# The start flag in place of a memset for the forward attention's accumulators

## The chip, the cores and the metric

The kernel runs on one core of a Trainium2 chip. The metric is the device time of one execution in microseconds (us). A ratio below is the mean time of one kernel's fast runs over that of the other's of the same rounds, with a 95% interval; so it is not quite the ratio of the medians that are quoted. The engines are PE (TensorE: matmuls, in program order), PEld (its weight loads), DVE (VectorE), ACT (ScalarE) and POOL (GpSimd). PSUM is the memory that the matmuls write, here the tile `accbank`, and a bank is one part of it; the start flag is a matmul's argument `start`. In the profile's timeline a row runs on over idle gaps under 0.15 us.

## The reference, cut to what matters

The whole is one transformer block, forward and backward: layer norm, attention with 32 heads of 16 columns over 2048 rows, an MLP, and the gradients. The change touches the forward attention alone:

```
qkv = (x @ wqkv).reshape(B, S, 3, H, Dh) ...        # S = 2048, H = 32, Dh = 16
p = softmax(einsum('bhqd,bhkd->bhqk', q, k) * scale)
o = einsum('bhqk,bhkd->bhqd', p, v)
```

## The kernel before

The forward works in 64 units: 4 chunks of 512 queries x 16 pairs of heads. A unit has 16 steps, one for each block of 128 keys. From one unit to the next there are 63 changes, which are numbered below. A step makes the score tile `st` on PE, the exponential `pu` on ACT, and, two steps later, the value product: eight matmuls that add `pu` times `Vaug` into eight groups of 17 columns (2 heads x 4 blocks of queries; column 17 sums the weights). After the last step DVE reads the unit out. Background work (projections, the MLP) is mixed in on PE between the steps.

```python
accp = self.open_pool("fwacc", bufs=1, space=PSUM)
accbank = accp.tile([P, 2, 2, 4, DH + 1], F32, name="accbank")    # two halves of one tile
...
def pv(u):
    (qc, g, jp, kb, acc, pu) = u
    if kb == 0:
        nc.vector.memset(acc, 0.0)
    for a in range(2):
        h = 4 * g + 2 * jp + a
        for sub in range(4):
            nc.tensor.matmul(acc[:, a, sub, :], lhsT=pu[:, a, sub * P:(sub + 1) * P], rhs=Vaug[:, kb, h, :],
                             start=False, stop=False, skip_group_check=True)
    if kb < ST - 1:
        return
    st0 = 4 * qc
    for a in range(2):                                            # the readout: four DVE instructions
        h = 4 * g + 2 * jp + a
        nc.vector.reciprocal(self.rl[:, st0:st0 + 4, h], acc[:, a, :, DH])
        nc.vector.tensor_tensor(O32[:, :, h * DH:(h + 1) * DH], acc[:, a, :, 0:DH],
                                self.rl[:, st0:st0 + 4, h:h + 1].to_broadcast([P, 4, DH]), ALU.mult)
    if (g, jp) == (NQ - 1, 1) and qc < SC - 1:
        bg.add(self.gen_mlp(qc, self.take_o(qc, O32)))            # four casts on DVE, then the MLP
...
for n, (qc, g, jp) in enumerate(order):
    acc = accbank[:, n % 2]
    for kb in range(ST):
        ...
        nc.tensor.matmul(stt[:, a, :], ...)                       # a = 0, 1: the scores
        nc.scalar.activation(pu[:], stt[:], ACT.Exp, scale=self.scale)
        pend.append((qc, g, jp, kb, acc, pu))
        if len(pend) > 2:
            pv(pend.pop(0))
        bg.step(1.08 if qc else 1.15)                             # background matmuls
```

The softmax here doesn't subtract the row's maximum and nothing guards it: scores larger than these inputs give would overflow.

## Time and profile before

| | kernel before |
|---|---|
| median of three runs | 3085.02 us (3082.49 to 3086.32) |
| time and span of the profiled run (not one of the three) | 3071.37 and 3069.6 us |
| first to last value matmul (start to start) | 110.2 to 1149.8 us |
| PE idle before a value matmul, for the memset | 64.1 us, 63 times |
| ACT idle before an exponential | 84.4 us |

The next lines are the view of busy time by stretches, for two stretches in the middle and at the end of the forward. Each engine's busy us has its count of instructions behind it; the last three columns are PE's granted clock, the DMA engines' busy share and GB/s.

```profile
370.00:650.00 280.00, 252.24 (x3064) 140.78 (x3117) 83.47 (x253) 263.10 (x283) 52.83 (x91) 0.98 0.37 91
900.00:1155.00 255.00, 229.44 (x2699) 125.90 (x2747) 76.84 (x238) 231.53 (x249) 43.66 (x76) 0.98 0.25 71
```

ACT (the fourth pair) is busy 263.10 of 280 us, 94%; the 17 us that it stands still there are what a change in this stage can win. DVE, on which the memset runs, is busy 30%.

### The profile page before, as it was taken

What the parts mean: (1) busy time and instruction counts of PE and PEld (TensorE: products, weight loads), DVE (VectorE), ACT (ScalarE), POOL (GpSimd) and SP (SyncE); (2) the same over time, 40 slices, a digit from 0 to 9 for tenths busy, and PEclk for the clock granted to TensorE, in tenths of its full rate; (3) what the DMA queues carried; (4) which work ended last, traced back from release to release, by engine and by line L of the source; (5) the groups of instructions that cost most, each with busy time, mean ns of one, the idle gap of its engine ahead of it and who ended that gap; (6) DMA issues with size and microseconds to landing.
All of it is one profiled execution on the core that took longest, in us unless ns stands there. A gap on an engine that the chain in (4) does not pass through costs nothing. (4 is left out here: it accounts for less than half of the span.)

```text
span 3069.6 us, 72394 instructions
## 1 busy us (share of the span) xinstructions
PE 2731.8 (89%) x29893; PEld 1417.4 (46%) x30394; DVE 1822.7 (59%) x2661; ACT 2240.1 (73%) x3322; POOL 396.6 (13%) x646
## 2 busy tenths in 40 slices
PE   3689889989998988589999999999999999999796
PEld 1345445544444543454444444444444444444343
DVE  5322123322322334367888888888888888888575
ACT  3489999999999984106777777777777777777443
POOL 2343111320221122571000000000000000000000
PEclk7899999999999999799999999999999999999898
DMA  3974230531351136888999999999999999999942
GB/s 128 212 166 121 65 88 25 141 80 37 93 114 48 54 99 183 177 195 164 188 205 200 188 204 189 201 194 192 205 191 206 195 194 206 188 188 180 235 128 72
DMA packets 1306719, 471.12 MB, mean 153 GB/s; under 512 B 1237074, under 2 KB 1269844, under 8 KB 1306388
## 3 DMA queue, kind: packets, MB, share of 16 engines
q1 hardware_dynamic: 1277476, 378.87, 65.7%
q0 software_dynamic: 28384, 86.01, 9.1%
q8 instruction: 238, 3.90, 0.5%
q10 hardware_dynamic: 528, 1.57, 0.1%
q14 instruction: 93, 0.76, 0.1%
HBM read 88.87 MB, written 67.64 MB: 51 GB/s over the span
## 5 line engine op out<-in xcount | busy, mean ns | idle before, releaser
L1185 ACT ACTIVATE pu<-st 128x512 bf16<-128x512 f32 x2048 | 1132.7, 597 | 361.0 <-PE st L1183 297.4
L1190 DVE TENSOR_TENSOR ds<-dp,pu 128x1024 bf16<-128x1024 f32 x1024 | 1208.1, 1219 | 232.9 <-ACT pu L1185 225.0
L361 ACT ACTIVATE pu<-st 128x1024 bf16<-128x1024 f32 x1024 | 956.8, 1047 | 84.4 <-PE st L358 80.4
L1183 PE MATMUL st<-KTm,QTq 128*128 128x512 bf16 x2048 | 778.3, 380 | 13.3 <-ACT pu L1185 11.5
L1133 PEld LDWEIGHTS <-dsT 128*128 128x128 bf16 x8192 | 486.7, 96 | 489.6 <-DMA dsT<-ds 20.2
L1186 PE MATMUL dp<-VTm,dOTq 128*128 128x512 bf16 x1779 | 672.6, 378 | 7.4 <-DVE ds L1190 6.0
L358 PE MATMUL st<-QTm,KTq 128*128 128x512 bf16 x1937 | 596.0, 384 | 57.9 <-issue 17.4
L1133 PE MATMUL accq<-Kg,dsT 128*128 128x16 bf16 x8192 | 493.2, 170 | 27.8 <-DMA dsT<-ds 13.5
L328 PEld LDWEIGHTS <-pu 128*128 128x128 bf16 x8192 | 355.7, 96 | 326.1 <-issue 95.9
L328 PE MATMUL accbank<-Vaug,pu 128*128 128x17 bf16 x8192 | 359.3, 171 | 70.0 <-DVE accbank L324 64.1
L1113 PE MATMUL acckv<-ds,Qg 128*16 128x512 bf16 x2048 | 308.3, 381 | 0.9 <-DVE ds L1190 0.7
L1113 PE MATMUL acckv<-pu,dOg 128*16 128x512 bf16 x2048 | 308.3, 381 | 0.0
L1183 PEld LDWEIGHTS <-QTq 128*128 128x128 bf16 x2048 | 195.9, 96 | 220.8 <-issue 215.8
L358 PEld LDWEIGHTS <-KTq 128*128 128x128 bf16 x2048 | 194.7, 97 | 214.7 <-issue 165.4
L1186 PEld LDWEIGHTS <-dOTq 128*128 128x128 bf16 x2048 | 197.3, 96 | 38.0 <-DVE ds L1190 16.2
L1044 POOL DMA_DIRECT2D wqkv<-in_A_wqkv_dram x1 | 0.8, 788 | 1493.1 <-DMA dsT<-ds 1493.1
L464 DVE TENSOR_SCALAR ev_fm<-pps,bcol 128x512 bf16<-128x512 f32 x60 | 45.0, 750 | 156.7 <-PE pps L456 88.7
L335 DVE RECIPROCAL rl<-accbank 128x4 f32<-128x4 f32 x128 | 23.0, 179 | 175.3 <-PE accbank L328 175.3
L309 POOL DMA_DIRECT2D QTm<-QTq_d x128 | 64.9, 510 | 450.0 <-PE st L358 406.4
L914 DVE TENSOR_SCALAR rT<-pps,bias 128x512 bf16<-128x512 f32 x42 | 31.5, 750 | 116.9 <-PE pps L911 116.7
L922 DVE SCALAR_TENSOR_TENSOR auT<-pps,rT 128x512 bf16<-128x512 f32 x42 | 29.0, 691 | 86.1 <-PE pps L920 71.0
L456 PE MATMUL pps<-xhat1T,wpad 128*128 128x512 bf16 x223 | 78.8, 393 | 0.3 <-issue 0.2
(313 smaller groups left out, 2125.1 us busy)
## 6 DMA issues: line engine op xcount, KB each, us to landing
KTq<-KTq_d POOLq DMA_DIRECT2D x32, 512.0 KB, 3.6
duT_d<-auT POOLq DMA_DIRECT2D x4, 1792.0 KB, 8.2
aT_d<-rT POOLq DMA_DIRECT2D x4, 1792.0 KB, 12.7
QTq_d<-ev_fm SPq DMA_DIRECT2D x32, 128.0 KB, 2.1
QTm<-QTq_d POOLq DMA_DIRECT2D x128, 32.0 KB, 2.0
KTq_d<-ev_fm SPq DMA_DIRECT2D x32, 128.0 KB, 2.0
VTq_d<-vT POOLq DMA_DIRECT2D x4, 1024.0 KB, 6.3
O_d<-O POOLq DMA_DIRECT2D x4, 1024.0 KB, 7.1
```

Of the source, the lines that this page charges most:

```text
L309: nc.gpsimd.dma_start(QTm[j][32 * j:32 * j + 32, :], self.QTq_d[g, 32 * j:32 * j + 32, 512 * qc:512 * (qc + 1)])
L328: nc.tensor.matmul(acc[:, a, sub, :], lhsT=pu[:, a, sub * P:(sub + 1) * P], rhs=Vaug[:, kb, h, :], start=False, stop=False, skip_group_che ...
L358: nc.tensor.matmul(stt[:, a, :], lhsT=KT[:, kb * P:(kb + 1) * P], rhs=QTm[2 * jp + a][:], start=True, stop=True)
L361: nc.scalar.activation(pu[:], stt[:], ACT.Exp, scale=self.scale)
L456: nc.tensor.matmul(pt[:], lhsT=self.wpads[t][:, kt, g, :], rhs=self.xhat1T[:, kt, s0:s0 + 512], start=(kt == 0), stop=(kt == DT - 1))
L464: nc.vector.tensor_scalar(ev[:], pt[:], bc, None, ALU.add)
L1113: nc.tensor.matmul(acckv[r:r + DH, :], lhsT=T[n][:, ib, col:col + DH], rhs=src[:, a, :], start=(ib == 0), stop=(ib == ST - 1))
L1133: nc.tensor.matmul(accq[:, ib, a, :], lhsT=dsT[:, (i * 2 + a) * 4 + sub, :], rhs=T["K"][:, 4 * c + sub, col:col + DH], start=(c == 0 and i ...
L1183: nc.tensor.matmul(stt[:], lhsT=T["QT"][:, q], rhs=masked["KT"][2 * jp + a][:, c0:c0 + 512], start=True, stop=True)
L1185: nc.scalar.activation(pu[:, a, :], stt[:], ACT.Exp, scale=self.scale)
L1186: nc.tensor.matmul(dp[:, a, :], lhsT=T["dOT"][:, q], rhs=masked["VT"][2 * jp + a][:, c0:c0 + 512], start=True, stop=True)
L1190: nc.vector.tensor_tensor(dsg[:, i], dp[:], pu[:], ALU.mult)
```

## The change

The intent is to drop the memset and let the first matmul of a unit, which carries the start flag, overwrite instead of adding.

```diff
         def pv(u):
             (qc, g, jp, kb, acc, pu) = u
-            if kb == 0:
-                nc.vector.memset(acc, 0.0)
             for a in range(2):
                 h = 4 * g + 2 * jp + a
                 for sub in range(4):
                     nc.tensor.matmul(acc[:, a, sub, :], lhsT=pu[:, a, sub * P:(sub + 1) * P], rhs=Vaug[:, kb, h, :],
-                                     start=False, stop=False, skip_group_check=True)
+                                     start=(kb == 0 and a == 0 and sub == 0), stop=False, skip_group_check=True)
```

## The prediction

> **What bounds the kernel now.** I read the page's forty slices first, to see whether the stage that the change touches has one limit.
>
> ```profile
> PE   3689889989998988589999999999999999999796
> DVE  5322123322322334367888888888888888888575
> ACT  3489999999999984106777777777777777777443
> ```
>
> The forward attention is slices 2 to 14, about 108 to 1150 us. There ACT is at 9 tenths nearly throughout, PE at 8 to 9, and DVE only at 1 to 3. So DVE's busy time is no cost in this stage, and removing DVE work can only pay where somebody waits for it. The backward stage after it (slices 18 to 37) is not touched; it can only start earlier or later. The next view is the groups by line, for 90 to 1155 us; its columns are operation, count, busy us and mean ns, then idle time before and what ended it.
>
> ```profile
> L361 ACT ACTIVATE pu<-st 128x1024 bf16<-128x1024 f32 x1024 | 956.8, 1047 | 84.4 <-PE st L358 80.4 <-ACT pu L361 0.5 <-remote 0.5
> L328 PE MATMUL accbank<-Vaug,pu 128*128 128x17 bf16 x8192 | 359.3, 171 | 70.0 <-DVE accbank L324 64.1 <-issue 0.4
> L336 DVE TENSOR_TENSOR O<-accbank,rl 128x64 f32<-128x64 f32 x128 | 28.4, 222 | 3.4 <-DVE rl L335 0.2
> L335 DVE RECIPROCAL rl<-accbank 128x4 f32<-128x4 f32 x128 | 23.0, 179 | 175.3 <-PE accbank L328 175.3
> L324 DVE MEMSET accbank<- 128x136 f32 x64 | 11.0, 172 | 5.9 <-DVE Vaug L441 0.2
> ```
>
> The reader should see three things. The exponentials (L361) are 956.8 us of a stage of some 1040 us: ACT is the limit, 14.95 us for each of the 64 head-pair units. ACT is idle for only 84.4 us before them, and 80.4 of that waits for the score matmuls (L358). And PE idles 64.1 us, in 63 of the 64 units, before the first value matmul of a unit (L328), waiting for the memset. PE works in program order, so while it stands at that matmul it cannot make the next score tile, and ACT runs dry. The 64.1 us looks like the prize. The timeline of one change of units shows that it is not.
>
> ```profile
> 617.19 0.23 DVE L336 TENSOR_TENSOR O<-accbank,rl 128x64 f32<-128x64 f32 x1
> 617.52 0.17 DVE L324 MEMSET accbank<- 128x136 f32 x1
> 617.74 0.35 PE L328 MATMUL accbank<-Vaug,pu 128*128 128x17 bf16 x8 [0.43 <-DVE accbank L324]
> ...
> 618.85 14.92 ACT L361 ACTIVATE pu<-st 128x1024 bf16<-128x1024 f32 x16 [0.35 <-PE st L358]
> ```
>
> Columns: start, length, engine, line, operation; in brackets the idle time before and its releaser. The memset is the last of five DVE instructions in a chain: PE ends the old unit, then reciprocal, multiply, reciprocal, multiply read it out, then the memset clears the other half of the same tile, then PE goes on. The last multiply ends at 617.42, the memset at 617.69, PE starts at 617.74. ACT then idles 0.35 us and runs 16 exponentials without a gap. This is the repeating pattern: one ACT bubble per unit, caused here.
>
> **What the Trainium skill says.** PSUM — Partial Sum Buffer, section The four PSUM rules: a matmul with the start flag clears the written bits of its whole 2 KiB bank on the quadrants it writes, and a later matmul without it overwrites where the bit is clear and adds where it is set. The accumulator tile is 2 halves x 136 fp32 = 1088 bytes, so both halves lie in one bank; one start flag per unit therefore prepares all eight 17-column groups, and the other half is already complete, because PE runs the units in order. So the result should stay right with no added matmul. The same page, section PSUM bank collisions raise a hardware error: two engines must not touch one bank and quadrant at once, even at different columns. Hence the new unit's first matmul must still wait until DVE has finished reading the old unit in the other half. The trace before agrees with ordering by the whole tile: the first reciprocal reads only head 0's half of the columns but starts after all eight matmuls of both heads; and the memset of the second unit, which clears a half that nobody has used, did not run in DVE's free time between 99.6 and 111.1 us but at 127.60, after the first unit's multiplies, while later work such as L855 was moved far ahead. Perfetto Trace Analysis, section Per-instruction lifecycle, says that a DVE record ends at the write acknowledgement, with the semaphore's travel after it. The trace fits: memset end to PE start is 0.05 us. I expect the same 0.05 after the multiply.
>
> **The change, part by part.** Removed: 64 memsets of 172 ns, 11.0 us of DVE busy time, worth nothing as such. Added: a flag on 64 of the 8192 matmuls; the shape stays 128x17, so no time. Moved: PE's wait, from the memset to the last multiply before it. What the path gains per unit is from the multiply's end to the memset's end: 617.69 - 617.42 = 0.27 us, of which 0.17 is the memset and 0.10 the gap between two DVE instructions. I took this difference for all 63 units from the timeline of DVE. In 53 it is 0.26 to 0.28 us. In ten it is 0.38 to 1.86 us, as other DVE work stands between: at the ends of the first three query chunks four casts (L865) of the finished output do.
>
> ```profile
> 379.24 1.62 DVE L865 CAST O_b<-O 128x512 bf16<-128x512 f32 x4
> ...
> 380.88 0.17 DVE L324 MEMSET accbank<- 128x136 f32 x1
> ...
> 381.11 0.36 PE L328 MATMUL accbank<-Vaug,pu 128*128 128x17 bf16 x8 [2.01 <-DVE accbank L324]
> ```
>
> Here PE waits 2.01 us and would be free of the casts: 1.85 us gained. The others sit behind one to three layer-norm or copy steps.
>
> Not each gain reaches the end: ACT is the limit, so PE's gain counts only as far as ACT was idle after it. For each unit I therefore took the smallest of three: the gain, PE's recorded wait, and ACT's idle time in the three microseconds after the memset. In 8 units ACT did not idle at all (0.43 us of PE wait was hidden by the two buffered score tiles); they give 0. The ten large ones give 10.8 us together. The other 45 give 12.2 us, some 0.27 each. Sum: 23.0 us. The recorded ACT idle time in these places is 61.6 us, so some 39 us of it stays: the two reciprocals and multiplies and whatever delays them.
>
> **Rivals.** (a) The wait is taken off altogether: if nothing orders the new half against reading the old one, up to the whole 64.1 us of PE wait goes, and of ACT's idle time up to 61.6 us: 3085 - 61.6 = 3023.4 us, exactly at the border of 2%. For it: the halves are disjoint in columns. Against it: the two signs of tile-wide ordering above, and the collision rule. I give it 4%. (b) ACT is the limit and the wait is hidden anyway: then about 0. For it: 8 units show precisely that, and ACT's digits are 9. Against it: a bubble of 0.35 us or more after most of the other memsets. A weaker form, where a third of the 0.27 us is given back to another wait, makes the gain some 15 us. (c) A new order: with the memset gone, the layout of other instructions on DVE and GpSimd may shift, so that a multiply lands behind a 0.7 us background operation more often; PE's long waits now (6.03 us at 193.38, 3.37 at 155.97, 3.10 at 957.10) come from late multiplies, not from the memset, and could grow or shrink by several us. This is noise of perhaps 8 us either way. (d) The earlier stage collides with DMA: I think not, as the DMA share is 0.25 to 0.37 between 370 and 1155 us.
>
> **Range and chances.** 3085.0 - 23.0 = 3062.0. Taking something off for given-back time (b), I predict 3064 us, -0.7%. With (c)'s 8 us and (b)'s weaker form, 3051 to 3077 should hold it 8 times in 10. Two per cent is 61.7 us, more than the sum by far; only (a) comes near. Slower by 2% would need a new wait of 1 us in every unit; nothing on PE was added.
>
> **What would show it.** Right: no L324 records; the same PE idle before L328, now released by the multiply (L336), about 64.1 - 25.2 = 39 us in total, where 25.2 is the sum of the gains bounded by PE's wait alone; a common wait of 0.16 instead of 0.43 us; ACT idle before L361 down from 84.4 to about 61; the backward stage unchanged in length. Wrong: PE's wait before L328 vanishing (rival a); ACT's idle time unchanged although PE's wait fell (b); multiplies standing behind other DVE work, with waits of over 1 us in more units than before (c).

## The result, and the profile after

The changed kernel takes 3055.51 us median (3054.82 to 3059.33, four runs) against 3084.86 us: ratio 0.9908 (0.9891 to 0.9925). The result is correct with one start flag for eight groups. On a second chip job it was 3054.74 against 3077.71 us, ratio 0.992, and on a third 3052.24 against 3077.98 us, ratio 0.9917; these two ran on one chip. So it is 23 to 29 us faster.

The groups by line of the changed kernel, 90 to 1155 us; the lines of the code are two lower than before (L359 was L361, L326 was L328, L334 was L336, L333 was L335):

```profile
L359 ACT ACTIVATE pu<-st 128x1024 bf16<-128x1024 f32 x1024 | 955.9, 1050 | 58.8 <-PE st L356 53.6 <-ACT pu L359 0.5 <-remote 0.5
L326 PE MATMUL accbank<-Vaug,pu 128*128 128x17 bf16 x8192 | 359.0, 171 | 47.1 <-DVE O L334 38.6 <-DVE lnb_nc L971 2.4 <-issue 0.7
L334 DVE TENSOR_TENSOR O<-accbank,rl 128x64 f32<-128x64 f32 x128 | 28.5, 222 | 3.1
L333 DVE RECIPROCAL rl<-accbank 128x4 f32<-128x4 f32 x128 | 23.0, 180 | 177.7 <-PE accbank L326 177.7
```

There is no memset row. PE's wait has a new releaser, the multiply of the readout (L334), and fell from 64.1 to 38.6 us; the 2.4 us put down to L971 (a small layer-norm step on DVE right behind the multiply) belong to it too, which makes 41.0. ACT's idle time fell from 84.4 to 58.8 us, by 25.6. The value matmul is 171 ns as before.

The same change of units as the prediction showed (the 31st), now in the changed kernel: the last multiply, PE's first value matmul of the new unit, and ACT's row over this stretch. Below it is ACT's busy time in 4 us around this change (stretch, length, busy us with the count, then the granted clock and the DMA's share and GB/s), first in the kernel before, then in the changed one.

```profile
607.43 0.23 DVE L334 TENSOR_TENSOR O<-accbank,rl 128x64 f32<-128x64 f32 x1
...
607.71 0.35 PE L326 MATMUL accbank<-Vaug,pu 128*128 128x17 bf16 x8 [0.16 <-DVE O L334]
...
589.09 34.65 ACT L359 ACTIVATE pu<-st 128x1024 bf16<-128x1024 f32 x37
```

```profile
616.00:620.00 4.00, 3.65 (x5) 1.00 0.43 125
606.00:610.00 4.00, 3.92 (x5) 1.00 0.43 124
```

The multiply ends at 607.66 and PE starts 0.05 us later; PE's wait is 0.16 instead of 0.43 us. ACT's row of 37 exponentials runs from 589.09 to 623.74 us, but it hides a short gap: ACT is busy 3.92 of 4 us where it was busy 3.65. So the bubble of 0.35 us at this change shrank to 0.08 us, by the same 0.27 us as PE's wait; it is not gone. In all 63 changes of this trace PE starts 0.05 to 0.06 us after the end of the last multiply.

At the end of a query chunk the four casts (here L863) now run beside PE:

```profile
375.06 0.23 DVE L334 TENSOR_TENSOR O<-accbank,rl 128x64 f32<-128x64 f32 x1
375.31 1.62 DVE L863 CAST O_b<-O 128x512 bf16<-128x512 f32 x4
...
375.33 0.35 PE L326 MATMUL accbank<-Vaug,pu 128*128 128x17 bf16 x8 [0.15 <-DVE O L334]
```

The wait here was 2.01 us and is 0.15 us. And the stretch of 280 us in the middle of the forward:

```profile
370.00:650.00 280.00, 259.84 (x3159) 145.14 (x3217) 81.56 (x238) 270.29 (x291) 52.84 (x91) 0.99 0.37 92
```

ACT is busy 270.29 of 280 us instead of 263.10, and PE gets 95 matmuls more done in the same time.

From the first value matmul's start to the last one's, the forward takes 1013.0 us (110.9 to 1123.9) instead of 1039.6, 26.6 us less. The profiled span fell by 16.1 us only. One reason is that the profiled run of the kernel before, 3071.37 us, was 11 us faster than the fastest timed one of that job (3082.49 us). Within the two traces, the difference lies between the stages: from the last value matmul to the first DVE step of the backward stage (the first `ds`) it is 251.6 us before and 257.9 after; from there to the span's end, 1668.2 and 1671.7. Over all traces that part between the stages varies from 251 to 262 us, so I take these few microseconds for scatter of single traces and judge the kernels by their timed runs.

### The profile page after: what moved, and what is told of

The parts are those of the page before. It is cut to its first block, busy times and chain, and to the rows that moved or that the text cites. A ratio compares the mean times of both kernels' runs of the same rounds, so it can differ in the third digit from the quotient of the medians.

```text
span 3053.5 us, 72311 instructions
## 1 busy us (share of the span) xinstructions
PE 2735.2 (90%) x29893; PEld 1420.6 (47%) x30394; DVE 1814.1 (59%) x2597; ACT 2238.9 (73%) x3322; POOL 396.4 (13%) x646
## 5 line engine op out<-in xcount | busy, mean ns | idle before, releaser
L359 ACT ACTIVATE pu<-st 128x1024 bf16<-128x1024 f32 x1024 | 955.9, 1050 | 58.8 <-PE st L356 53.6
L326 PEld LDWEIGHTS <-pu 128*128 128x128 bf16 x8192 | 355.4, 96 | 302.5 <-issue 71.9
L326 PE MATMUL accbank<-Vaug,pu 128*128 128x17 bf16 x8192 | 359.0, 171 | 47.1 <-DVE O L334 38.6
L333 DVE RECIPROCAL rl<-accbank 128x4 f32<-128x4 f32 x128 | 23.0, 180 | 177.7 <-PE accbank L326 177.7
```

## The experiments

All ten runs were correct, and each stands beside runs of the kernel before on the same chip.

**1. The change again.** Comment lines keep the line numbers; the code is the change's.

> The change again (line numbers kept by comment lines), to get its time against the kernel before on one chip, with more rounds. Theory (the start of the first value matmul moves from the memset's end to the last multiply's end): about 3055 us, ratio 0.991, PE idle before the value matmuls 41 us against 64 us. Rival (part of the 29 us was a better draw of the chip, since the profiled spans differ by 16 us only): ratio 0.994 to 0.995.

Measured: 3054.74 us (3052.11 to 3056.06) against 3077.71; ratio 0.992 (0.9904 to 0.9935). PE idle 42.3 us (39.9 + 2.4). So 0.991 is inside and 0.994 just outside the interval: the gain is real in timed runs, though the kernel before was 7 us faster here than in the first job, so that part of the first job's 29 us stays unconfirmed.

**2. The flag without the gain.** The flag is set and the memset stays.

```diff
-                                     start=False, stop=False, skip_group_check=True)
+                                     start=(kb == 0 and a == 0 and sub == 0), stop=False, skip_group_check=True)
```

> The start flag is set but the memset stays; the order of instructions on all five engines is that of the kernel before. Theory: as before, ratio 1.000 within 0.2%, PE idle before L328 64 us, released by the memset. Rival (the flag makes the matmuls cheaper, or overwriting instead of adding does): some of the 29 us is gained, ratio below 0.997, the 128x17 matmul under 171 ns.

Measured: 3078.99 us, ratio 0.9998 (0.9984 to 1.0013); the matmul is 171 ns; PE waits 60.3 us for the memset. The flag by itself gains nothing. Since the order of instructions is the same as before, this trace is also a second trace of the kernel before for every purpose of time: the two differ by 3.8 us in PE's wait and by 4.4 us in the length of the forward.

**3. The memset kept, but ahead of what stood between.**

```diff
-            if kb == 0:
+            if kb == 0 and (qc, g, jp) == order[0]:
                 nc.vector.memset(acc, 0.0)
...
+            if (qc, g, jp) != order[-1]:
+                nc.vector.memset(accbank[:, (order.index((qc, g, jp)) + 1) % 2], 0.0)
             if (g, jp) == (NQ - 1, 1) and qc < SC - 1:
```

> The kernel before with each memset issued right behind the last multiply of the unit before, ahead of the casts and of the background work that stood between in ten units; no flag; otherwise the same order on all engines. Theory (53 units cost 0.27 us each, ten cost more through what stands between): the ten units' excess over 0.27 us is gained, 10.8 - 10 x 0.27 = some 8 us: ratio 0.9974, 3077 us; PE idle before L328 about 55 us. Rival (the memset itself costs all, what stands between is hidden): ratio 1.000.

Measured: 3069.44 us, ratio 0.9972 (0.9956 to 0.9988). The time is as expected (with a wide interval: 3.7 to 13.5 us gained), PE's wait fell less: to 58.5 us. The trace says why: of the ten units, the three with casts went from 2.01, 2.00 and 1.85 to 0.43, 0.44 and 0.28 us and one other from 2.18 to 1.52, while the remaining six kept their waits, as the placing of DVE's instructions still put a background step ahead of the memset there. So the casts in front of the memset cost 1.6 us each, and PE's wait on them was not hidden.

**4. The memset twice.**

```diff
-            if kb == 0:
+            for _ in range(2 if kb == 0 else 0):
                 nc.vector.memset(acc, 0.0)
```

> The kernel before with each memset done twice, so that the chain is 0.2 to 0.27 us longer in all 63 units. Theory (the chain of readout and memset sets when ACT gets its next score tile, and each tenth of a microsecond of it counts): 55 to 63 units x 0.2 to 0.27 us = 11 to 17 us more, ratio 1.0036 to 1.0055, PE idle before L328 about 77 to 81 us. Rival (the wait is mostly hidden behind ACT, and the change gained elsewhere): under 4 us, ratio below 1.0013.

One change of units, with the last multiply, both memsets and PE's restart:

```profile
938.97 0.23 DVE L336 TENSOR_TENSOR O<-accbank,rl 128x64 f32<-128x64 f32 x1
939.29 0.45 DVE L324 MEMSET accbank<- 128x136 f32 x2
...
939.79 0.35 PE L328 MATMUL accbank<-Vaug,pu 128*128 128x17 bf16 x8 [0.70 <-DVE accbank L324]
```

From the multiply's end (939.20) to the second memset's end (939.74) it is 0.54 us; with one memset it was 0.27. Each memset thus costs the chain 0.27 us, not its 172 ns, and PE's wait of 0.43 became 0.70. In sum PE waits 83.2 us, 21 more than the mean of the two traces with one memset (62.2). Measured time: 3105.77 us (3090.89 to 3112.26), ratio 1.0084 (1.0063 to 1.0105): 28 us more by the medians. That is more than the expected 17. ACT's idle time is 102.4 us against their mean of 82.1, so 20.3 of the 21.0 us reached ACT. The profiled run, the fastest of the six at 3090.89 us, has a forward 20 us longer than the mean of those two traces (1057.9 against 1037.4). The other five were 13 to 21 us slower than it and have no trace; their granted clock was 0.962 to 0.965 against its 0.969, which may be why, but nothing here shows it. The rival (hidden) falls.

**5. The change a third time**, as the base for the next three.

> The changed kernel once more, as the base for the three runs beside it on this chip. Ratio to the kernel before 0.991 to 0.992.

Measured: 3052.24 us, ratio 0.9917 (0.9901 to 0.9934); PE's wait 44.4 us, ACT's idle time 55.3 us.

**6. A shorter readout on top of the change.**

```diff
-            for a in range(2):
-                h = 4 * g + 2 * jp + a
-                nc.vector.reciprocal(self.rl[:, st0:st0 + 4, h], acc[:, a, :, DH])
-                nc.vector.tensor_tensor(O32[:, :, h * DH:(h + 1) * DH], acc[:, a, :, 0:DH],
-                                        self.rl[:, st0:st0 + 4, h:h + 1].to_broadcast([P, 4, DH]), ALU.mult)
+            h = 4 * g + 2 * jp
+            rlv = self.rl[:, st0:st0 + 4, h:h + 2].rearrange("p s a -> p a s")
+            nc.vector.reciprocal(rlv, acc[:, :, :, DH])
+            nc.vector.tensor_tensor(O32[:, :, h * DH:(h + 2) * DH].rearrange("p s (a d) -> p a s d", a=2), acc[:, :, :, 0:DH],
+                                    rlv.unsqueeze(3).to_broadcast([P, 2, 4, DH]), ALU.mult)
```

> The changed kernel, with the readout of both heads in one reciprocal and one multiply instead of two each. Theory (what is left of PE's wait is the readout chain): the chain is some 0.3 to 0.35 us shorter, and the smallest of that, PE's wait and ACT's idle time, summed over the units of the changed kernel's trace, is 7.9 to 9.0 us: ratio to the changed kernel 0.997, PE idle before the value matmuls some 42 - 20 = 22 to 30 us. Rival (in most units the wait is hidden behind ACT by now, and the long ones come from other DVE work in front): under 3 us.

The groups of this kernel (90 to 1160 us) and one readout:

```profile
L361 ACT ACTIVATE pu<-st 128x1024 bf16<-128x1024 f32 x1024 | 951.6, 1054 | 40.8 <-PE st L358 36.1 <-remote 2.2 <-ACT pu L361 0.5
L328 PE MATMUL accbank<-Vaug,pu 128*128 128x17 bf16 x8192 | 358.1, 171 | 22.5 <-DVE O L336 16.0 <-issue 0.2
...
601.23 0.21 DVE L335 RECIPROCAL rl<-accbank 128x8 f32<-128x8 f32 x1 [6.74 <-PE accbank L328]
601.47 0.29 DVE L336 TENSOR_TENSOR O<-accbank,rl 128x128 f32<-128x128 f32 x1
```

The readout takes 0.53 us (601.23 to 601.76) instead of 0.80 (606.86 to 607.66), and PE waits over 0.15 us in 20 changes only, 16.0 us in all. Measured: 3036.73 us (3032.78 to 3041.52), ratio to the kernel before 0.9863, so 15.5 us below the changed kernel where 8 to 9 were expected. The readout was indeed most of what was left of the wait. The sum was too small mostly because of the long waits, which it held constant: by the changes' own records, PE waited 14.7 us at the second to fourth change in run 5 and 7.0 here, and 2.82 and 0 at the 52nd. At the second and the 52nd the last multiply stood behind other DVE work in run 5, and here it does not. But run 7, with the four instructions, has 7.4 us at the second to fourth change too, so that part of the gain may be scatter.

**7 and 8. The two halves in two banks.** The PSUM is full, so run 7 first takes a buffer from the background matmuls, as a control, and run 8 uses it.

```diff
-        self.mps = self.open_pool("mps", bufs=3, space=PSUM)
+        self.mps = self.open_pool("mps", bufs=2, space=PSUM)
--- and for run 8 also ---
-        accbank = accp.tile([P, 2, 2, 4, DH + 1], F32, name="accbank")
+        accbank = [accp.tile([P, 2, 4, DH + 1], F32, name=f"accbank{i}") for i in range(2)]
-                acc = accbank[:, n % 2]
+                acc = accbank[n % 2][:]
```

> Control for the next: the changed kernel with two instead of three PSUM buffers for the background matmuls, which frees a bank. Theory: background groups are four or more matmuls apart, DVE is lightly loaded, so little is lost: 0 to 10 us slower than the changed kernel. Rival: PE waits for evacuation in the stretches of dense background work, 20 us or more.

> As the control, with the two accumulator halves as tiles of their own in two banks; the start flag as in the change. Theory (the wait that is left, 42 us of PE and 37 us of ACT behind it, is there because both halves share one bank, so that reading the old unit and writing the new one are ordered): PE idle before the value matmuls falls to under 5 us and the time to 25 to 37 us below the control. Rival (the order comes from elsewhere, such as the value matmul's other inputs, or ACT hides it): within 5 us of the control.

The same two groups in run 8:

```profile
L361 ACT ACTIVATE pu<-st 128x1024 bf16<-128x1024 f32 x1024 | 950.6, 1057 | 32.3 <-PE st L358 27.9 <-remote 1.7 <-ACT pu L361 0.5
L328 PE MATMUL accbank<-Vaug,pu 128*128 128x17 bf16 x8192 | 358.4, 171 | 7.1 <-issue 0.7
```

The row of the value matmuls has no DVE releaser any more. One change of units (the 31st again), the last multiply of the old unit and PE's first value matmuls of the new one:

```profile
598.04 0.23 DVE L336 TENSOR_TENSOR O<-accbank,rl 128x64 f32<-128x64 f32 x1
...
598.01 0.35 PE L328 MATMUL accbank<-Vaug,pu 128*128 128x17 bf16 x8
```

PE now starts before the multiply does; in 62 of the 63 changes it starts before the multiply has ended. Measured: run 7 3062.63 us (3042.00 to 3071.68, a wide spread whose cause is open), ratio 0.9937, 10.4 us above run 5 and so just past the 0 to 10 that were expected; run 8 3026.42 us (3022.17 to 3038.06), ratio 0.9837. Run 8 is 36.2 us below its control by the medians, at the upper end of what was expected. As the control scatters, two steadier figures stand beside it: in the traces the forward is 26.9 us shorter than the control's (981.3 against 1008.2), and the median is 25.8 us below run 5. So the wait that the change left is there because both halves are one tile in one bank: with a tile and a bank for each half, PE begins the new unit while DVE reads the old one. Run 8 changes tile and bank together, so it does not tell which of the two makes the order.

**9 and 10. Both together, and run 8 again.**

> Two banks for the halves and the joint readout together. Theory (both act on the same wait, and with two banks PE no longer waits at all): no further gain over the two banks alone, 3020 to 3032 us, within 0.3% of the run beside it. Rival (the joint readout also gains by itself, as a shorter readout on DVE): another 5 us or more below it.

> The halves in two banks once more, as the base for the run beside it: ratio to the kernel before 0.982 to 0.986.

Measured: 3025.41 us (ratio 0.9836) with the joint readout, 3025.99 us (0.9841) without. The two remedies do not add: once PE does not wait, the length of the readout is of no consequence. ACT is still idle for 31.7 and 34.2 us before its exponentials; that rest has other causes, which were not studied. Both kernels beat the change by some 26 us, though not on the same chip; run 8, beside run 5, gave 25.8.

## Why the prediction was right, point by point

- **The removed wait was 0.27 us per unit, not the recorded 1 us.** Right. PE starts 0.05 us after the multiply as it did after the memset, and the common wait went from 0.43 to 0.15 or 0.16 us. The test by doubling gives the same 0.27 us per memset.
- **PE's wait in total.** Forecast about 39 us; measured 41.0, 42.3 and 44.4 us in three traces. Broken up by changes of units, with run 1 for the changed kernel: the ten with other work between went from 19.0 to 8.2 us, a gain of 10.8, and the prediction's sum for them was 10.8. Fifty-one of the other 53 went from 35.8 to 21.4 us, 0.28 each. The second and fourth change grew from 9.4 to 12.7 us. Those two have late multiplies, in the first query chunk, where the order on POOL and SP changed; run 2, with the order of before, had 5.6 us there. The prediction spoke of a background operation of 0.7 us in front; most of the time here is DVE's own wait. The readout stands behind a copy out of PSUM (`ev_fm`), and before that copy DVE stands still for a DMA (`ev_tm<-ev_fm`), 5.97 and 4.43 us at these two changes in the first trace after. So this is the scatter that rival (c) named, and whether the new order or chance made it is not separated.
- **ACT passes the gain on.** Right, and a little better than assumed: ACT's idle time was forecast to be about 61 us and came to 58.8, 55.9 and 55.3 us. The forward stage shrank by 26.6 us in the first pair of traces; the mean of three traces after (1010.5) and two with the memset kept (1037.4) gives 26.9. The sum was 23.0. One misreading made it too small: it gave nothing to eight units in which ACT seemed not to idle. At seven of these changes ACT's records do have a gap, of 0.13 us, which the timeline's rows hide; after the change it is gone at all seven. That adds 0.9 us; the other 3 stay open.
- **The time.** 3064 was forecast, 3055.51 came, in the range. The sum of 23.0 agrees with the 23 us and 25.7 us of the second and third job and is 6 us short of the first. I had taken 2 us off for gains given back to other waits; no such loss shows in the forward stage. The timed runs of the kernel before scatter by job (medians 3085 and 3078 us), and I have no trace of a slow one, so the last few microseconds stay open. Among its runs of the second job the slowest, 3086.49 us, had a granted clock of 0.965 and the fastest, 3072.07 us, 0.969; whether the clock makes the scatter was not tested.
- **The rivals.** (a) The wait did not vanish with one tile for both halves: PE starts right behind the multiply in all 63 changes. Run 8 shows that it does with a tile and a bank for each. (b) It was not hidden: run 4 shows that ACT loses nearly all of each tenth that PE waits (20.3 of 21.0 us). (d) No collision with DMA shows in the stretch from 370 to 650 us, where its share is 0.37 both times; the long waits behind a DMA, above, are in the first query chunk, one of them in the kernel before too (4.98 us at the fourth change).
- **The Trainium skill.** That one start flag prepares all groups of the bank (PSUM — Partial Sum Buffer, section The four PSUM rules) held, as the results are correct. The same page's collision rule cannot be tested here; what the runs show is that the program keeps the order within the one tile, and not between two.

## What to carry to other kernels

When an engine waits for the last instruction of a chain, removing that instruction wins only the stretch back to the one before it, here 0.27 of a mean 1.02 us; find the end of the next-to-last instruction in the timeline, and cap the gain by the idle time of the engine that sets the pace. Look at what has come to stand in front of a small instruction too: the casts in front of it, three times 1.6 us, were a fifth of the forecast gain. And two halves of one PSUM tile are no double buffer if their reader and their writer are kept in order: a tile and a bank for each half were worth about as much again as the removed memset (25.8 us below run 5, which was 25.7 us below the kernel before).

## What the Trainium skill lacked or had wrong

- PSUM — Partial Sum Buffer, section The four PSUM rules, gives the start flag on the first matmul and the memset to zero as two idioms that both work. It does not say what the memset costs on the path: 0.27 us per reuse of the accumulator here (172 ns of work, 0.10 us between two DVE instructions), 0.8 to 0.9% of the whole time together with the work that queued up in front of it.
- Perfetto Trace Analysis, section Matmuls, advises that independent groups should rotate through different banks. Run 8 agrees with it. The section gives no size: here 26 us against the changed kernel and 36 against the control, 0.8 to 1.2% of this kernel, for 63 changes of accumulator.
- Perfetto Trace Analysis, section Per-instruction lifecycle, leaves the semaphore's travel after a DVE instruction without a figure. From the end of a DVE record to the start of a PE matmul that waits for it, these traces show 0.05 us, the same after a memset and after a multiply; it holds the travel and whatever else PE does before its record starts.
